# Turning two normalised tiles ahead of K's first half at the head of an attention kernel

## The chip, the cores and the metric

The kernel runs on one core of one Trainium2 chip. The metric is the device time of one execution in microseconds (us). Each execution also has a span: first to last instruction as the hardware profiler saw it, about 1.8 us shorter.

## The reference

Layer normalisation of x (2048 x 640), 32 heads of attention with head size 192 over given K and V caches, an output projection, and a gated feed-forward network whose silu scales the attention output. Everything is bf16.

```python
xn = _layernorm(x)
q = (xn @ wq)                       # per head: 2048 x 192
p = softmax(q @ k_cache.T * 192 ** -0.5)
s = concat_heads(p @ v_cache) @ wo
g = silu((silu(xn @ w1) * (xn @ w3)) @ w2)
return x + s * g
```

## The kernel before

One long stream of score and value products fills TensorE. In front of it stands a head of some 14 us, which loads, normalises and transposes what the first scores need. TensorE transposes by multiplying with an identity; the result goes to PSUM, the memory for TensorE's results (`pk` and `pst` in the timelines), and ScalarE or VectorE copies it out. In the timelines below ScalarE, VectorE and TensorE do their work in the order in which the program emits it (ScalarE, say: K at 9.00, the x tiles at 9.91). A load "lands" when its last byte has arrived. These are the parts of the head that the change touches:

```python
def turn_over(k):                   # products of the identity with itself: they keep TensorE's clock up
    for i in range(k):
        nc.tensor.matmul(warm, lhsT=ident_bf[:], rhs=ident_bf[:], start=True, stop=True)

def turn_k0(dst, half, sel):        # transposes of head 0's K, four per entry of sel     (L271)
def copy_k0(copy, src, half, two):  # copies half of them to KW                           (L277)
def ln_norm(g, i, engine):          # normalises tile i of x block g                      (L346)
def ln_turn(g, i2, copy):           # transposes two normalised tiles (L354), copies them to xnT (L356)
# ... cut ...
def head_start():
    load_x(0, 0, 2)
    load_x(0, 2, 4)
    load_k0(0, nc.sync)             # K, first half
    load_w0()
    turn_over(34)
    # ... cut: statistics of the four tiles; loads of K's second half, x block 1, V's first half ...
    for i in range(4):
        ln_norm(0, i, nc.vector)
    pk0 = ps_o.tile([P, 4, 512], BF16, tag="ob0", name="pk0")
    turn_k0(pk0, 0, range(4))                  # 16 transposes of K
    copy_k0(nc.scalar.copy, pk0, 0, 0)
    turn_over(4)
    ln_turn(0, 0, nc.scalar.copy)              # tiles 0 and 1
    turn_k0(pk1, 1, (0, 1))
    ln_turn(0, 1, nc.vector.tensor_copy)       # tiles 2 and 3
    swap_halves(0)
    copy_k0(nc.scalar.copy, pk0, 0, 1)
    copy_k0(nc.vector.tensor_copy, pk1, 1, 0)
    load_v(0, (1,))                            # V, second half
    load_x(2)                                  # the third block of x
    project_first()                            # first projection: q of head 0 (L391)
    turn_k0(pk1, 1, (2, 3))
    copy_k0(nc.scalar.copy, pk1, 1, 1)
    scores(0)                                  # first score products (L483)
    shift_first()                              # copies of q on VectorE (L400, L401)
    shift_k0()                                 # a copy of K on VectorE (L281)
    scores(1)
    ln_stats(1, 0)                             # statistics of the second block, then of the third (L316)
    # ... cut ...
```

## Time and profile before

| | before |
|---|---|
| time, median of the first 3 runs | 1941.45 us (1940.62 to 1942.42) |
| span of the profiled execution | 1939.6 us |
| TensorE busy | 1928.9 us |
| first projection product starts | 11.20 us |
| first score product starts | 14.06 us |

Three lines of the page of the kernel before: span, busy time of the engines, and, by engine, the chain of work that ended last (followed back from the last instruction to what each step waited for).

```profile
span 1939.6 us, 59659 instructions
...
PE 1928.9 (99%) x27267; PEld 1317.8 (68%) x27275; DVE 654.2 (34%) x997; ACT 1181.2 (61%) x1278; POOL 282.6 (15%) x501
...
PE 98%; DVE 1%; DMA 0%; ACT 0%; issue 0%; SPq 0%; POOL 0%; DVEq 0%; ACTq 0%
```

TensorE fills nearly all of the span and the chain. Only in the head can anything be won by moving work about.

The timeline of the head, cut to the instructions in question. Columns: start and duration in us, engine, line, operation, written tile <- read tiles, shape, number of instructions merged, and in brackets how long the engine was idle and what ended it.

```profile
2.77 3.81 PE L569 MATMUL pk<-ident_bf 128*128 128x128 bf16 x34 [2.77 <-POOL ident_bf masks.py:199]
...
7.14 0.79 DVE L346 TENSOR_SCALAR xn<-x_all,mv,rstd 128x640 bf16<-128x640 bf16 x2
...
7.90 1.07 PE L271 MATMUL pk<-ident_bf,kn 128*128 128x128 bf16 x16 [1.32 <-DMA kn<-in_A_k_cache_dram]
...
9.00 1.01 ACT L277 COPY KW<-pk 128x1024 bf16<-128x1024 bf16 x1 [2.85 <-PE pk L271]
9.03 0.72 PE L354 MATMUL pst<-ident_bf,xn 128*128 128x128 bf16 x10
...
9.91 1.23 ACT L356 COPY xnT<-pst 128x1280 bf16<-128x1280 bf16 x1
...
11.20 2.34 PE L391 MATMUL ps<-xnT,W 128*128 128x256 bf16 x20 [0.44 <-ACT xnT L356]
...
14.06 0.39 PE L483 MATMUL st<-qA,KW 128*128 128x512 bf16 x1
...
22.12 0.88 DVE L316 BATCH_NORM_STATS2 stats<-x_all 128x6 f32<-128x320 bf16 x2
```

The 34 products start 107 ns apart, the last at 6.27 (the 3.81 us also hold the end of the last one). The 16 transposes of K start when K lands and follow each other every 56 ns. ScalarE copies K first (9.00) and the two x tiles after it (9.91), and the first projection (11.20) waits for the second copy. The last line is VectorE's start on the third block of x.

The chain of waits of the kernel before, in its head (start, duration, what):

```profile
1.68 6.17 DMA kn<-in_A_k_cache_dram
7.90 1.08 PE pk L271 x16
9.00 1.01 ACT KW L277
10.02 1.14 ACT xnT L356
11.20 2.36 PE ps L391 x20
```

It says the same: the landing of K's first half, K's transposes, two copies on ScalarE, the projection.

### The profile page before, as it was taken

Reading aid. Unit: us, or ns where it says so; the run is one execution under the profiler, and the core shown is the slowest. Engines: PE = TensorE matmul, PEld = TensorE weight load, DVE = VectorE, ACT = ScalarE, POOL = GpSimd, SP = SyncE. Lnnn points to the kernel's source line nnn. Section 1 sums busy time; section 2 is a strip of 40 time slices with the busy share of each in tenths; the row PEclk is TensorE's granted clock in tenths of the full one; section 3 lists DMA queues with packets and bytes.
Section 4 is the critical chain, followed back from the end, with each engine's and each line's share of the span. In section 5 each row is a group of like instructions: output and inputs, shape, how many; then the busy total and the mean of one; then the engine's idle time right before and its main releaser. Section 6 shows DMA issues by size and latency. Waiting matters only on the chain.

```text
span 1939.6 us, 59659 instructions
## 1 busy us (share of the span) xinstructions
PE 1928.9 (99%) x27267; PEld 1317.8 (68%) x27275; DVE 654.2 (34%) x997; ACT 1181.2 (61%) x1278; POOL 282.6 (15%) x501
## 2 busy tenths in 40 slices
PE   8999999999999999999999999999999999999998
PEld 6666666666666666666666666666666666577776
DVE  7333333333333333333333333333333334521111
ACT  6667676767776767776777777677767677210000
POOL 3111111111111111111111111111111110000000
PEclk9999999999999999999999999999999999999999
DMA  8643433323233434363434343434333220937882
GB/s 178 132 101 64 101 68 83 86 56 91 58 89 65 98 63 99 68 162 68 101 64 101 68 101 68 100 66 100 69 68 90 63 70 2 259 70 135 152 152 61
DMA packets 394643, 178.98 MB, mean 92 GB/s; under 512 B 341616, under 2 KB 382832, under 8 KB 394384
## 3 DMA queue, kind: packets, MB, share of 16 engines
q1 hardware_dynamic: 371136, 125.32, 30.9%
q0 software_dynamic: 19472, 45.71, 9.8%
q8 instruction: 215, 3.52, 0.8%
q10 hardware_dynamic: 3776, 4.06, 0.7%
q14 instruction: 44, 0.36, 0.1%
HBM read 52.82 MB, written 27.79 MB: 42 GB/s over the span
## 4 chain that ended last, share of the span: by engine, by line
PE 98%; DVE 1%; DMA 0%; ACT 0%; issue 0%; SPq 0%; POOL 0%; DVEq 0%; ACTq 0%
PE obank L516 35%; PE st L487 33%; PE ps L424 14%; PE ps_s L111 11%; PE ps_f L728 3%; PE ps_gu L702 1%; PE st L488 1%; PE ps L410 0%; DMA kn<-in_A_k_cache_dram 0%; DVE stats L316 0%; PE ps L391 0%; DVE xn L346 0%; DVE mv L317 0%; DVE qA L429 0%; ACT xnT L356 0%
## 5 line engine op out<-in xcount | busy, mean ns | idle before, releaser
L490 ACT ACTIVATE pT<-st 128x1024 bf16<-128x1024 f32 x1024 | 1047.1, 1023 | 251.1 <-PE st L488 235.6
L516 PEld LDWEIGHTS <-pT 64*128 64x128 bf16 x16384 | 713.7, 94 | 242.2 <-ACT pT L490 0.2
L516 PE MATMUL obank<-vt,pT 64*128 64x193 bf16 x16384 | 851.8, 243 | 0.0
L487 PE MATMUL st<-qC,KW 64*128 64x512 bf16 x2046 | 605.6, 376 | 0.1
L525 DVE COPY osum<-obank 128x772 f32<-128x772 f32 x128 | 123.1, 962 | 788.8 <-PE obank L516 788.8
L488 PE MATMUL st<-qB,KW 64*128 64x512 bf16 x1024 | 385.0, 376 | 0.0
L487 PE MATMUL st<-qA,KW 64*128 64x512 bf16 x1022 | 384.3, 376 | 0.4 <-ACT pT L490 0.3
L488 PE MATMUL st<-qC,KW 64*128 64x512 bf16 x1022 | 384.3, 376 | 0.0
L488 PE MATMUL st<-qA,KW 64*128 64x512 bf16 x1022 | 384.3, 376 | 0.0
L487 PEld LDWEIGHTS <-KW 64*128 64x128 bf16 x3068 | 278.0, 94 | 153.8 <-issue 2.1
L424 PE MATMUL ps<-xnT,W 64*128 64x512 bf16 x1280 | 297.2, 376 | 0.0
L424 PE MATMUL ps<-xnS,W 64*128 64x512 bf16 x1280 | 296.3, 376 | 0.0
L488 PEld LDWEIGHTS <-KW 64*128 64x128 bf16 x3068 | 278.0, 94 | 0.7 <-issue 0.6
L377 POOL DMA_DIRECT2D qC<-qA x124 | 65.4, 528 | 1285.6 <-DVE rl_all L532 1270.0
L430 ACT CAST qB<-ps 128x512 bf16<-128x512 f32 x131 | 76.8, 586 | 228.3 <-PE ps L424 222.7
L111 PE MATMUL ps_s<-wo_sb,oT 128*128 128x384 bf16 (+3 forms) x1535 | 208.8, 299 | 0.1
L424 PEld LDWEIGHTS <-W 64*128 64x128 bf16 x2560 | 122.9, 94 | 121.2
L111 PEld LDWEIGHTS <-oT 128*128 128x128 bf16 x1536 | 148.4, 98 | 60.4
L526 DVE TENSOR_TENSOR osum<-osum,obank 128x772 f32<-128x772 f32 x128 | 122.7, 958 | 13.4
L533 DVE TENSOR_TENSOR ostage<-osum,rl_all 128x768 bf16<-128x768 f32 x128 | 122.7, 958 | 4.4
L465 DVE SCALAR_TENSOR_TENSOR hT<-pt,qB 64x512 bf16<-64x512 bf16 x64 | 43.8, 684 | 199.4 <-ACT pt L464 199.4
L429 DVE CAST qA<-ps 128x512 bf16<-128x512 f32 x131 | 90.5, 691 | 25.2 <-PE ps L410 7.2
(84 smaller groups left out, 622.4 us busy)
## 6 DMA issues: line engine op xcount, KB each, us to landing
o_scr<-ostage SPq DMA_DIRECT2D x16, 1536.0 KB, 10.3
vt<-in_A_v_cache_dram SPq DMA_DIRECT2D x63, 384.0 KB, 5.7
qC<-qA POOLq DMA_DIRECT2D x248, 64.0 KB, 1.9
qC<-qB POOLq DMA_DIRECT2D x124, 64.0 KB, 2.4
wo_sb<-in_A_wo_dram POOLq DMA_DIRECT2D x1, 7680.0 KB, 36.2
W<-in_A_wq_dram POOLq DMA_DIRECT2D x32, 160.0 KB, 3.4
W<-in_B_w_dram POOLq DMA_DIRECT2D x32, 80.0 KB, 3.2
W<-in_A_wq_dram POOLq DMA_DIRECT2D x32, 80.0 KB, 2.9
```

The lines of the kernel that those rows point to most:

```text
L111: nc.tensor.matmul(ps[:, 0:w], lhsT=oT[:, k, :], rhs=wo_sb[:, k, c0:c1], start=(k == 0), stop=(k == OC - 1))
L377: nc.gpsimd.dma_start(out=qC[0:64, half, :], in_=qAB[half][64:P, :])
L424: nc.tensor.matmul(ps[:, r * 512:(r + 1) * 512], lhsT=W[rows, j, :], rhs=xs[rows, j // 2, qs], start=(j == 0), stop=(j == 2 * DC - 1))
L429: a = nc.vector.tensor_copy(out=qAB[0][:], in_=ps[:, 0:512])
L430: b = nc.scalar.copy(out=qAB[1][:], in_=ps[:, 512:1024])
L487: nc.tensor.matmul(st2[:, 0:512], lhsT=ka, rhs=qa, start=r == 0 and nr == 3, stop=r == nr - 1)
L488: nc.tensor.matmul(st2[:, 512:1024], lhsT=kb, rhs=qb2, start=r == 0 and nr == 3, stop=r == nr - 1)
L490: nc.scalar.activation(out=pT2[:], in_=st2[:], func=ACT.Exp, scale=att_scale)
L516: nc.tensor.matmul(obanks[r][:, j * 256:j * 256 + DH + 1], lhsT=pT2[r * 64:(r + 1) * 64, t * 512 + j * P:t * 512 + (j + 1) * P], rhs=vt[r ...
L525: nc.vector.tensor_copy(out=osum[:], in_=ov[0])
L526: nc.vector.tensor_tensor(out=osum[:], in0=osum[:], in1=ov[1], op=ALU.add)
L533: nc.vector.tensor_tensor(out=ostage[:, qb * 4:qb * 4 + 4, hg * DH:(hg + 1) * DH], in0=osum[:, :, 0:DH], in1=rl.unsqueeze(2).to_broadcast( ...
```

## The change

The intent: turn the first two x tiles while K is still landing, let ScalarE copy them first, and keep TensorE busy with clock-keeping products until the first tile is normalised, so that the four filler products behind K's transposes are no longer needed.

```diff
-        turn_over(34)
+        turn_over(44)
 ...
         pk0 = ps_o.tile([P, 4, 512], BF16, tag="ob0", name="pk0")
+        ln_turn(0, 0, nc.scalar.copy)
         turn_k0(pk0, 0, range(4))
+        ln_turn(0, 1, nc.vector.tensor_copy)
+        turn_k0(pk1, 1, (0, 1))
+        swap_halves(0)
         copy_k0(nc.scalar.copy, pk0, 0, 0)
-        turn_over(4)
-        ln_turn(0, 0, nc.scalar.copy)
-        turn_k0(pk1, 1, (0, 1))
-        ln_turn(0, 1, nc.vector.tensor_copy)
-        swap_halves(0)
         copy_k0(nc.scalar.copy, pk0, 0, 1)
```

## The prediction

> **What bounds the kernel now.** The page shows TensorE busy for 1928.9 of 1939.6 us, and the chain of what ended last is 98% TensorE. The change can only act in the first 14 us of this; its real idle time lies there. The work behind it is unchanged, so at most part of the head can be won, under 0.1%.
>
> **The head, from the timeline.** The 34 clock-keeping products start at 2.77 us and are spaced 107 ns; the last one starts at 6.27. The transposes of K's first half start at 7.90, when that load lands (7.85), and are spaced 56 ns. The Trainium skill ("TensorE: Matmul & The Clock Gate", Part 1) gives the same two spacings for a throttled and a free array, 106.7 and 55.6 ns. The trace agrees; the clock opens between 6.4 and 7.9 us. On TensorE then follow in order: 16 K transposes, 4 filler products, 10 transposes of normalised tiles 0 and 1 (9.03), 8 K transposes, 10 of tiles 2 and 3 (10.03, last starts 10.54). ScalarE copies K out first (9.00, 1.01 us) and the first x tiles only after it (9.91, 1.23 us). So the first projection (L391) waits for that copy and starts at 11.20, with 0.44 us of TensorE idle. The chain of waits runs the same way.
>
> **What the change does.** Tiles 0 and 1 are normalised at 7.58 and 7.94. Their 10 transposes now go first, as K lands: last result about 8.45. ScalarE copies xnT at once, 8.5 to 9.7 instead of 9.91 to 11.14. TensorE: K's 16 about 8.3 to 9.15; tiles 2 and 3 (normalised by 9.07) to 9.7; VectorE copies them 9.9 to 10.7 instead of 10.79 to 11.62; 8 K transposes to 10.2. The projection can start at about 10.2, 1.0 us earlier. The 10 added products run where TensorE idles: 3 at 107 ns and 7 at 56, ending at about 7.3, ahead of the first norm; they cost nothing. ScalarE's two KW copies now follow the xnT copy (9.7 to 11.75), delaying its first cast of q a little but not the scores. First scores: about 13.1 instead of 14.06; first exponential about 14.0 instead of 15.05.
>
> **How much survives.** DMA does not speed up: the windows show it about fully busy from 10 to 22 us, so loads issued earlier land hardly earlier. The third block of x landed at 21.82 and VectorE began on it at 22.12, only 0.3 us later; behind it in VectorE's order stands the cast of the next q (23.16), for which TensorE waits at 23.86. The swapped x landed at 19.00 and is read at 20.07. So between 0.3 and 1.0 us should survive to the steady stage, where TensorE hides nothing and gives it all to the end. I expect about 0.7 us off: 1940.7 us, with 8 chances in 10 for 1939.4 to 1941.9. Faster by over 2%: 0.003; within: 0.99; slower: 0.007.
>
> **What would show it.** L354 before L271 on TensorE at about 7.6; L391 starting near 10.2; first L483 near 13.1; first L490 near 14.0; score matmuls at 36 us 0.3 to 1.0 us earlier.
>
> **What would make it wrong.** The clock opening late or closing again, so that the head runs at 107 ns (costing about 1 to 2 us); the projection held by another wait, such as the second K load (9.22); the third x load swallowing all the gain; run-to-run scatter above the effect.

## The result, and the profile after

| | before | after |
|---|---|---|
| median, 6 runs each | 1941.93 us (1940.62 to 1942.85) | 1941.61 us (1940.53 to 1941.92) |
| span of the profiled execution | 1939.6 | 1938.7 |
| first projection product | 11.20 | 10.31 |
| first score product | 14.06 | 13.26 |

The ratio is 0.9998, with a 95% interval of 0.9985 to 1.0011: the same. A ratio here is the mean time of one kernel's fast runs over that of the other's in the same rounds, so it is not quite the ratio of the medians quoted. By time alone nothing is seen. By the two profiles, the change won 0.9 us. But a profile shows one execution: the one of the changed kernel took 1940.53 us, the fastest of all its eleven (the other ten: 1941.37 to 1941.93), while the one of the kernel before took an ordinary 1941.37.

Two lines of the page of the kernel after:

```profile
span 1938.7 us, 59672 instructions
...
PE 98%; DVE 1%; DMA 0%; ACT 0%; issue 0%; POOL 0%; DVEq 0%; ACTq 0%
```

The timeline of its head, same columns:

```profile
2.77 4.81 PE L569 MATMUL pk<-ident_bf 128*128 128x128 bf16 x44 [2.77 <-POOL ident_bf masks.py:199]
...
7.27 0.79 DVE L346 TENSOR_SCALAR xn<-x_all,mv,rstd 128x640 bf16<-128x640 bf16 x2
...
7.76 0.81 PE L354 MATMUL pst<-ident_bf,xn 128*128 128x128 bf16 x10 [0.18 <-DVE xn L346]
...
8.41 1.06 PE L271 MATMUL pk<-ident_bf,kn 128*128 128x128 bf16 x16
8.61 1.23 ACT L356 COPY xnT<-pst 128x1280 bf16<-128x1280 bf16 x1 [2.29 <-PE pst L354]
...
9.73 1.94 ACT L277 COPY KW<-pk 128x1024 bf16<-128x1024 bf16 x2
...
10.31 2.35 PE L391 MATMUL ps<-xnT,W 128*128 128x256 bf16 x20
...
13.26 0.38 PE L483 MATMUL st<-qA,KW 128*128 128x512 bf16 x1 [0.16 <-DVE qA L393]
...
21.24 0.88 DVE L316 BATCH_NORM_STATS2 stats<-x_all 128x6 f32<-128x320 bf16 x2
```

The order is as intended: x tiles (7.76), K (8.41); ScalarE copies x at 8.61 and K's pieces at 9.73; the projection starts at 10.31 without any idle time in front. The chain of waits in the head of the kernel after:

```profile
0.75 2.97 DMA x_all<-in_A_x_dram
...
7.35 0.37 DVE xn L346
...
7.76 0.81 PE pst L354 x10
8.57 0.89 PE pk L271 x16
...
10.47 2.20 PE ps L391 x20
```

It starts at the landing of x, not of K, and runs through the statistics, the norms and TensorE's own row. Matching the same instruction in both traces, the first score product is 0.80 us earlier, and from 23.6 us to the last product every one is 0.88 us earlier: nothing is given back in this pair of profiles.

### The profile page after: what moved, and what is told of

Same layout as the page of the kernel before. It is cut to its first block, busy times and chain, and to the rows that moved or that the text cites. A ratio compares the mean times of both kernels' runs of the same rounds, so it can differ in the third digit from the quotient of the medians.

```text
span 1938.7 us, 59672 instructions
## 1 busy us (share of the span) xinstructions
PE 1929.6 (100%) x27273; PEld 1318.5 (68%) x27281; DVE 654.0 (34%) x997; ACT 1180.2 (61%) x1278; POOL 282.6 (15%) x501
## 4 chain that ended last, share of the span: by engine, by line
PE 98%; DVE 1%; DMA 0%; ACT 0%; issue 0%; POOL 0%; DVEq 0%; ACTq 0%
PE obank L516 35%; PE st L487 33%; PE ps L424 14%; PE ps_s L111 11%; PE ps_f L727 3%; PE ps_gu L701 1%; PE st L488 1%; DVE stats L316 0%; PE ps L410 0%; DMA x_all<-in_A_x_dram 0%; DVE xn L346 0%; PE ps L391 0%; PE pst L354 0%; DVE mv L317 0%; PE pk L271 0%
## 5 line engine op out<-in xcount | busy, mean ns | idle before, releaser
L429 DVE CAST qA<-ps 128x512 bf16<-128x512 f32 x131 | 90.5, 691 | 25.2 <-PE ps L410 7.3
```

The lines of the kernel that those rows point to most:

```text
L429: a = nc.vector.tensor_copy(out=qAB[0][:], in_=ps[:, 0:512])
```

## The experiments

Twelve kernels ran, on three chips, each with five timed rounds beside the kernel before (six times for before_28). Every interval of a ratio is about plus or minus 0.0013 wide, which is 2.5 us. So no ratio here tells two of these kernels apart. The profiles and the lists of single times are the evidence. "Third block" is the load of the third block of x, and "101st value product" is a fixed landmark in the stream, behind which the order of work is the same in all kernels.

### The two kernels again, and the change in halves

The kernel before and the kernel after were run unchanged. Two kernels take one half of the change each:

```diff
 order_only  = after  with  -turn_over(44)  +turn_over(34)
 warm_only   = before with  -turn_over(34)  +turn_over(44)
```

> The kernel before once more, to see what varies by itself. Theory A (the order: the gain of 0.88 us seen in the two profiles is the earlier copy of the first x tiles): the first projection product starts again within 0.25 us of 11.2 us, whatever the landing of K's first half, because K's transposes, ScalarE's copy of K and its copy of xnT stand in a row behind that landing. Theory L (luck of a load: K's first half landed at 7.85 in the profile before and at 7.36 after): with an early landing near 7.4 the projection starts near 10.8 and half the gain is gone. Theory C (clock): the opening of the clock differs from 6.7 us, and where it opens later than 8 us the transposes run at 107 ns and the projection starts after 12 us. Timed ratio 1.000 by construction.

> The changed kernel once more. Theory A: first projection near 10.3 us and the score matmuls of the steady stage 0.8 to 0.9 us ahead of a profile of the kernel before with the same clock and landings; timed 0.3 to 0.9 us less than before, ratio 0.9995 to 0.9998, which may not be clear of the scatter of about 1 us. Theory L: the projection start moves with the landing of K. Theory C: the times scatter less than those of before, and the clock opens before 8 us in every profile.

> The new order with the 34 clock-keeping products of before instead of 44. TensorE then has nothing between 6.4 us and the first norm at about 7.7 us. Theory A: the head is the same as after the whole change, first projection near 10.3 us, as long as the clock opens before 7.7. Theory C: the longer idle leaves the clock closed through the transposes: spacing 107 ns, first projection 1 to 2 us later, near 12 us, in some runs or all.

> The kernel before with 44 clock-keeping products in place of 34 and nothing else changed. Theory A: no gain, first projection 11.0 to 11.3 us; the last product ends at about 7.6 us, ahead of K's landing or up to 0.2 us after an early one. Theory C: most of the gain is here, steady stage 0.5 us or more earlier, and the spread of the times shrinks.

Measured, medians of 5 against 1941.27 us of the kernel before (9 runs): before_again 1941.22, after_again 1941.80, order_only 1941.28, warm_only 1941.80.

In this second profile of the kernel before, K's first half landed at 7.31 us, not 7.85, and the projection started at 10.65, not 11.20. So theory A's first forecast, 11.2 whatever the landing, failed. Theory L is right as far as it goes: in four profiles with the old order and an open clock (before, before_again, warm_only and, below, before_x2_early) the first score product comes 6.2 us after K's landing (7.85 to 14.06, 7.31 to 13.51, 7.45 to 13.65, 7.34 to 13.54). With the new order and many clock-keeping products it stands at 13.2 to 13.3 whether K lands at 5.68 or 7.68. So in these profiles the head gain is 0.2 to 0.85 us, depending on a landing, and the first pair had shown nearly its upper end. It may be less: in four other profiles (order_only, after_x2_early, turn_order_only, before_cold) K landed at 5.68 to 6.22, from the same issue at 1.68 or 1.69, and no profile shows the old order with so early a landing and an open clock.

In after_again that gain reached the first score product (13.21) and was gone at the 101st value product, which came at 30.43 against 30.35 in the first profile of before. VectorE's timeline in after_again:

```profile
22.20 0.89 DVE L316 BATCH_NORM_STATS2 stats<-x_all 128x6 f32<-128x320 bf16 x2 [0.93 <-DMA x_all<-in_A_x_dram]
...
23.24 0.64 DVE L429 CAST qA<-ps 128x512 bf16<-128x512 f32 x1
```

And TensorE's next work behind that cast, in the same run:

```profile
23.94 0.73 PE L354 MATMUL pst<-ident_bf,xn 128*128 128x128 bf16 x10 [0.87 <-DVE qA L429]
```

VectorE had nothing to do for 0.93 us, because the third block of x had not landed. Behind that in VectorE's row stands the cast of the next q (L429), for which TensorE waited 0.87 us. The chain of waits of the same run:

```profile
13.54 8.64 DMA x_all<-in_A_x_dram
```

VectorE's start on the third block in order_only:

```profile
21.95 0.89 DVE L316 BATCH_NORM_STATS2 stats<-x_all 128x6 f32<-128x320 bf16 x2 [0.55 <-DMA x_all<-in_A_x_dram]
```

There the wait was 0.55 us, and in warm_only 0.47. In the first profile of after it was zero, with 0.09 us to spare: landing at 21.15, start at 21.24.

The extra products by themselves (warm_only) do not move the head: the projection started 3.34 us after K's landing, as before. Nor did the times draw together, as theory C had it: they lie between 1941.45 and 1943.20. Without them (order_only) the projection started at 10.38, practically as after. In the profiled executions the clock opened in time in both.

### The third block loaded earlier

```diff
-        load_v(0, (1,))
-        load_x(2)
+        load_x(2)
+        load_v(0, (1,))
```

> The changed kernel with one swap: the load of the third x block is issued ahead of the second half of V, not behind it. Theory X (the change does win about 0.85 us, but in the runs where the third x block lands later than about 21.2 us VectorE waits for it and the gain is given back): the block lands between 19.7 and 21.0 us, VectorE's wait in front of the third block's statistics is zero, the 101st value product starts at the first score product plus 16.2 us, near 29.5, and the timed median falls 0.4 to 1.0 us below before, with less scatter. Rival theory A0 (the change wins nothing outside its first profile, for another reason): a median as before, 1941.2 to 1941.9, though the block lands early.

> The kernel before with the same swap of the two loads and nothing else. Theory X: before, VectorE reached the third block at 21.6 to 22.1 us by its own pace, so early data gain only in executions where the block lands later than that: 0 to 0.4 us in the median, and less than the swap gains in the changed kernel; first score product still 13.5 to 14.1 us. Rival: if loads alone set the time, the same 0.4 to 1.0 us as in the changed kernel.

Measured against 1941.12 us of before (9 runs, mean 1941.42): after_x2_early 1940.77 (mean 1941.06; single times 1940.51, 1940.75, 1940.77, 1941.45, 1941.84), before_x2_early 1940.87 (mean 1941.34; 1940.14, 1940.71, 1940.87, 1942.40, 1942.56). The timeline of after_x2_early, the two loads and VectorE's start on the third block:

```profile
12.46 1.77 SPq L214 DMA_DIRECT2D x_all<-in_A_x_dram  x1
...
14.27 0.90 SPq L289 DMA_DIRECT2D vt<-in_A_v_cache_dram  x1
...
21.31 0.88 DVE L316 BATCH_NORM_STATS2 stats<-x_all 128x6 f32<-128x320 bf16 x2
```

The block landed at 20.39, VectorE did not wait, and the 101st value product came at 29.54, 16.20 us after the first score product, as theory X had it. In before_x2_early the block landed only at 21.13, outside what I had expected of an early issue, but before VectorE reached it at 21.60; the head was unchanged (first score product 13.54). The means fell by 0.36 and 0.08 us. The median of after_x2_early fell by 0.35 us, just short of the 0.4 to 1.0 expected, that of before_x2_early by 0.25 (expected 0 to 0.4). The order between the two is the expected one, the sizes are within the scatter. Two of the five times of after_x2_early (1941.45, 1941.84) are as slow as the changed kernel's usual ones, and no profile shows why.

### Which of the two orders matters

copy_order_only leaves TensorE's order as before and lets ScalarE copy x first. turn_order_only has TensorE's new order and lets ScalarE copy K first.

```diff
 copy_order_only (against before)
-        copy_k0(nc.scalar.copy, pk0, 0, 0)
         turn_over(4)
         ln_turn(0, 0, nc.scalar.copy)
+        copy_k0(nc.scalar.copy, pk0, 0, 0)
 turn_order_only (against after)
-        ln_turn(0, 0, nc.scalar.copy)
+        first = []
+        ln_turn(0, 0, lambda out, in_: first.append((out, in_)))   # transposes only
         turn_k0(pk0, 0, range(4))
+        copy_k0(nc.scalar.copy, pk0, 0, 0)
+        nc.scalar.copy(out=first[0][0], in_=first[0][1])
 ...
         swap_halves(0)
-        copy_k0(nc.scalar.copy, pk0, 0, 0)
```

> The kernel before with TensorE's order kept, and ScalarE's copy of the first x tiles put ahead of its copy of K. The x tiles' transposes still stand behind K's and the four fillers, so the x copy can start only about 0.5 us after K's landing plus 1.4 us. Both theories of a joint effect: first projection only 0.1 to 0.25 us earlier than before at the same landing of K (start 3.1 to 3.25 us after the landing, where before it was 3.34), first score product about unchanged. If ScalarE's order alone made the gain: projection near 10.3 us.

> The changed kernel with TensorE's new order, but ScalarE copies K first and the x tiles second, as before. The x tiles are turned by 8.5 us and then wait for ScalarE's copy of K, which can start only at about 9.5. Joint effect: first projection near 11.6 us, later than before in both profiles, first score product near 14.6, the 101st value product near 30.8, time 0.3 to 1.0 us more than the kernel before. If TensorE's order alone made the gain: projection near 10.3 us.

The timeline of copy_order_only:

```profile
9.55 1.23 ACT L356 COPY xnT<-pst 128x1280 bf16<-128x1280 bf16 x1 [3.10 <-PE pst L354]
...
10.82 2.35 PE L391 MATMUL ps<-xnT,W 128*128 128x256 bf16 x20 [0.31 <-ACT xnT L356]
```

The timeline of turn_order_only:

```profile
7.94 0.81 PE L354 MATMUL pst<-ident_bf,xn 128*128 128x128 bf16 x10 [0.44 <-DVE xn L346]
...
9.68 1.01 ACT L277 COPY KW<-pk 128x1024 bf16<-128x1024 bf16 x1 [3.17 <-PE pk L271]
...
10.59 1.23 ACT L598 COPY xnT<-pst 128x1280 bf16<-128x1280 bf16 x1
...
11.87 2.34 PE L391 MATMUL ps<-xnT,W 128*128 128x256 bf16 x20 [1.22 <-ACT xnT L598]
```

turn_order_only has the x tiles turned early and does not copy them until 10.59, behind K. Its projection starts at 11.87, later than in either profile of before, with 1.22 us of TensorE idle. Its times, 1941.91 to 1942.11, hardly scatter; their median is 0.82 us over that of before (expected 0.3 to 1.0). In copy_order_only the x tiles are turned behind K, and the projection starts at 10.82 with K landed at 7.20. That is 3.62 us after the landing, more than the 3.1 to 3.25 expected; the clock opened only at 8.16 in this execution, and the first nine gaps between K's transposes were 82 to 108 ns in place of some 56, which is 0.4 us of it. Its first score product came at 13.78, no better than before. Its single times were 1940.47, 1940.98, 1942.36, 1942.48 and 1942.62 (mean 1941.78). So neither order alone gives the early projection; both together do.

### What a late clock costs

```diff
 after_cold  = after  with  -turn_over(44)  +turn_over(1)
 before_cold = before with  -turn_over(34)  +turn_over(1)
 before_28   = before with  -turn_over(34)  +turn_over(28)
```

> The changed kernel with one clock-keeping product in place of 44, to price a clock that opens late. Claim of the change (products must keep the clock up to the first norms): the 44 transposes ahead of the projection run at 107 ns in place of 56 ns (2.2 us more), the projection starts near 12.6 us and the first products of it are slow too; the clock opens between 10.5 and 14.5 us; first score product 15.5 to 18; time 2 to 4 us over the kernel before. Rival: the chain waits elsewhere anyway, and the late clock costs under 0.5 us.

> The kernel before with one clock-keeping product in place of 34. It prices a late clock for the old order. The kernel before shows two clusters of times, about 1941.1 and about 1942.6. If the upper one is executions in which the clock opens [...]after K's transposes began, this kernel should lie at or above the upper cluster, 1942.5 to 1944.5, with no execution near 1941. If the clock is not the cause of the upper cluster and costs nothing, the same 1941.1 with the same two clusters.

> The kernel before with 28 clock-keeping products in place of 34, ending near 5.8 us in place of 6.4. It asks where the upper cluster of the kernel before comes from: 1942.2 to 1942.9 in about a third of its executions, and in none of the changed kernel's. Theory C2 [...]: with a longer pause most executions, 3 to 5 of 5, land at 1942.2 to 1944, the clock opening between 9 and 12.6 us where the profiled one is such an execution; any other stays near 1941.1. Rival (the cluster comes from loads that land late): still about 1 or 2 of 5 above 1942.2, and a clock opening that does not go with them.

Measured: after_cold 1943.75 (1943.56 to 1944.20) and before_cold 1943.97 (1942.84 to 1944.66), both against 1941.41 of before. In the trace's clock record the clock opens at 13.35 and 11.69 us, and the first score products come at 15.86 and 15.44. So the clock-keeping products are worth some 2.3 to 2.6 us in either order; 34 of them already earn that in most executions. Of the price, 0.5 to 0.9 us fell late: TensorE waited once more, for the transposed rows of the third block in front of a later projection (L410), 0.90 us until 42.67 in after_cold and 0.48 until 41.91 in before_cold (the rows landed 0.25 and 0.24 us before; in before_cold the profile puts the wait down to an exponential that ended at 41.90).

The kernel before has 39 executions, 11 of them between 1942.3 and 1942.9 and the others between 1940.6 and 1942.2. The changed kernel has 11, none above 1941.93. before_28 was to tell whether that upper cluster is a late clock. Its profiled execution took 1942.62 us; the timeline of TensorE in it:

```profile
7.78 1.89 PE L271 MATMUL pk<-ident_bf,kn 128*128 128x128 bf16 x16 [1.83 <-DMA kn<-in_A_k_cache_dram]
...
9.88 1.27 PE L354 MATMUL pst<-ident_bf,xn 128*128 128x128 bf16 x10
...
11.47 0.72 PE L354 MATMUL pst<-ident_bf,xn 128*128 128x128 bf16 x10
```

The 16 transposes of K take 1.89 us, 107 ns each, and only the last ten (11.47) are all at 56 ns; the clock record opens at 11.10. The first score product comes at 15.33. So an execution with a late clock does land in the upper cluster. But the count went against theory C2, that a longer pause behind the products makes most executions slow: only 2 of 6 executions lay above 1942.2, not 3 to 5 of 5, beside 4 of 10 of the kernel before on the same chip. Whether the upper cluster of the kernel before itself is late clocks is therefore not shown: no profile caught one of its slow executions.

### A version meant to beat both

x2_pool is after_x2_early with two copies moved from VectorE's row to GpSimd, which has nothing to do there.

```diff
     def shift_k0():
-        nc.vector.tensor_copy(out=KW[0:64, 3, :], in_=KW[64:P, 0, :])
+        nc.gpsimd.tensor_copy(out=KW[0:64, 3, :], in_=KW[64:P, 0, :])
     def shift_first():
-        nc.vector.tensor_copy(out=qC[0:64, 0, :], in_=qAB[0][64:P, :])
+        nc.gpsimd.tensor_copy(out=qC[0:64, 0, :], in_=qAB[0][64:P, :])
 ...
         copy_k0(nc.vector.tensor_copy, pk1, 1, 0)
-        load_v(0, (1,))
+        shift_k0()
         load_x(2)
+        load_v(0, (1,))
 ...
         shift_first()
-        shift_k0()
```

> A version that should beat both: the changed kernel, the third x block loaded ahead of V's second half, and two copies that stand in VectorE's row ahead of the second block's statistics (the shifted K, 0.42 us, and one half of the shifted q, 0.29 us) given to GpSimd, idle there. Theory (from 12.7 us on VectorE's row is what the steady stage waits for, unless the third block lands late): the second block's statistics start about 0.6 us earlier relative to the first score product, and the 101st value product comes about 15.6 us after the first score product in place of 16.2, unless the third block (19.7 to 21.0) now lands too late for it; timed 0.6 to 1.4 us under before. Rival: scores wait for GpSimd's slower copies, or VectorE and GpSimd hinder each other, and nothing is gained.

Measured: 1940.46 us (1940.29 to 1940.76) against 1941.41 (1940.96 to 1942.80); ratio 0.9994, interval 0.9981 to 1.0008. The five single times lie all below the nine of before. The timeline of x2_pool:

```profile
11.60 1.03 POOL L281 COPY KW<-KW 64x1024 bf16<-64x1024 bf16 x1 [1.15 <-ACT KW L277]
...
13.12 0.73 POOL L401 COPY qC<-qA 64x512 bf16<-64x512 bf16 x1 [0.48 <-DVE qA L393]
...
13.41 0.59 DVE L400 COPY qC<-qA 64x512 bf16<-64x512 bf16 x1
...
14.03 0.89 DVE L316 BATCH_NORM_STATS2 stats<-x_all 128x6 f32<-128x320 bf16 x2
```

The same copy in after_x2_early, where GpSimd copies nothing:

```profile
13.54 0.29 DVE L400 COPY qC<-qA 64x512 bf16<-64x512 bf16 x1
```

The third block landed at 20.53 and VectorE reached it at 20.82, 7.62 us after the first score product in place of 7.98. The hope of 0.6 us was cut twice. First, VectorE's remaining copy (L400) took 0.59 us in place of 0.29 while GpSimd made its own copy. The Trainium skill ("SBUF — State Buffer", "SBUF: two separate sides") says that VectorE and GpSimd share a port pair under an exclusive lock, in some of VectorE's modes. The trace fits that: L400 ended at 14.00, 0.15 us behind GpSimd's copy; which mode VectorE was in, no run shows. Secondly, of those 0.36 us only 0.12 reached the 101st value product (16.08 us after the first score product in place of 16.20), since TensorE, which in the other kernels waits for VectorE there, now began the next transposes (22.79) 0.29 us after VectorE's cast had ended (22.50), with 0.1 us of pause behind the value products, and had become the limit itself. How the rest of the lower times divides between the loads' order and scatter is not shown.

### All profiles in one table

Times in us, read from the traces of the profiled executions. "Clock opens" is the start of the first entry of the trace's clock record.

| kernel | clock opens | first score product | third block lands | VectorE starts on it (idle before) | 101st value product | span |
|---|---|---|---|---|---|---|
| before | 6.73 | 14.06 | 21.82 | 22.12 (0) | 30.35 | 1939.60 |
| before_again | 6.85 | 13.51 | 21.11 | 21.57 (0) | 29.80 | 1938.99 |
| after | 7.38 | 13.26 | 21.15 | 21.24 (0) | 29.47 | 1938.67 |
| after_again | 6.47 | 13.21 | 22.18 | 22.20 (0.93) | 30.43 | 1939.67 |
| order_only | 5.82 | 13.34 | 21.92 | 21.95 (0.55) | 30.18 | 1939.42 |
| warm_only | 6.82 | 13.65 | 22.25 | 22.27 (0.47) | 30.50 | 1939.74 |
| after_x2_early | 8.13 | 13.34 | 20.39 | 21.31 (0) | 29.54 | 1938.74 |
| before_x2_early | 6.89 | 13.54 | 21.13 | 21.60 (0) | 29.83 | 1939.10 |
| copy_order_only | 8.16 | 13.78 | 21.19 | 21.75 (0) | 29.98 | 1939.21 |
| turn_order_only | 7.21 | 14.73 | 21.60 | 22.79 (0) | 31.02 | 1940.28 |
| after_cold | 13.35 | 15.86 | 21.53 | 23.84 (0) | 32.07 | 1942.42 |
| before_cold | 11.69 | 15.44 | 21.23 | 23.51 (0) | 31.74 | 1941.59 |
| before_28 | 11.10 | 15.33 | 22.22 | 23.39 (0) | 31.62 | 1940.85 |
| x2_pool | 5.87 | 13.20 | 20.53 | 20.82 (0) | 29.28 | 1938.52 |

One rule fits all rows but x2_pool, which took work out of VectorE's row: VectorE starts on the third block at the later of two times, 8.0 to 8.1 us after the first score product, or the block's landing; 8.23 us after that start comes the 101st value product. And in every row but the two cold ones the span ends 1909.2 to 1909.3 us after that product (the cold ones took 0.6 and 1.1 us longer, mostly in the wait at L410 told above). So the span of a profiled execution with an open clock, to 0.1 us, is set by whichever of these two came last.

## Why the prediction was right or wrong

**The range and the class were right.** 1941.61 us lies in 1939.4 to 1941.9, and the kernel is neither faster nor slower by 2%. That much is luck: the range also holds 1941.45, the time of the kernel before, so no gain at all would have landed in it, and the point of 1940.7 was 0.9 us too low.

**The mechanism in the head was right.** L354 went first (7.76; predicted 7.6), the projection started at 10.31 (10.2), the first score product at 13.26 (13.1), the first exponential at 14.24 (14.0). copy_order_only and turn_order_only show that it takes both orders.

**The clock was right in its effect.** I let 7 of the 10 added products run at 56 ns; nearly all ran at 107, because the clock opened at 7.38. They still ended before the first tile was ready (TensorE stood idle for 0.18 us in front of L354), and cost nothing in that execution.

**"How much survives: between 0.3 and 1.0 us, about 0.7" is the term that failed**, in two ways. First, the 1.0 us by which the projection was to start earlier was counted against a single landing of K, at 7.85 us. That landing is not a constant: it was 7.31, 7.34 and 7.45 in three other profiles of the old order with that load unchanged, where the head gain to the first score product is 0.2 to 0.4 us. Secondly, I had named the third block as a possible limit with only 0.3 us of margin, and then let it cost a part of the gain. It took 0.93 us of VectorE's time in the second profile of the changed kernel, which swallowed the whole. The statement that "loads issued earlier land hardly earlier" held: with the original order of the loads the third block was issued between 13.5 and 16.2 us and landed between 21.1 and 22.3, and the earliest issue landed among the latest. Putting it in front of another load brought it to 20.39 and 20.53, and in before_x2_early only to 21.13.

**The steady time.** The kernel before has 39 executions with a mean of 1941.56 us, and the changed kernel 11 with a mean of 1941.59. The difference of 0.88 us between the first two profiles was real in those two executions and is not what the change does on average. What it does show is less spread: no execution above 1941.93 against 11 of 39 above 1942.3. The lists of the other kernels tell what this goes with. Where TensorE turns K first, as before, 19 of 60 executions lie above 1942.2 us (before 11 of 39, warm_only 1 of 5, before_x2_early 2 of 5, copy_order_only 3 of 5, before_28 2 of 6). Where it turns the x tiles first (after, order_only, after_x2_early, turn_order_only, x2_pool), none of 31 does; the slowest took 1942.11. The two cold kernels are left out. So the slow executions go with TensorE's order. Neither the ten added products nor the order of the loads nor ScalarE's order removed them by itself. Whether a late clock or a late K makes them is not shown.

**What stays open.** The changed kernel's typical execution (1941.4 to 1941.9) is slower than the lower cluster of the kernel before (27 executions from 1940.6 to 1941.7, mean 1941.12); the two means agree only because the upper cluster is gone. A late third block explains it in the one profile of the changed kernel that shows it, and in order_only, a relative of it; the executions without a profile leave no landing times. Why that load lands anywhere between 21.1 and 22.3 us is settled by half. The traces show that with the original order of the loads it landed 1.56 to 1.66 us after V's second half, which stands in front of it on the same queue, in ten of eleven profiles (before_cold: 1.85), whenever it had been issued. With the loads swapped, V's second half landed 1.29 to 1.31 us after it. That fits a load which takes its turn behind the other one, and says why an earlier issue alone did not help. Why that one landed anywhere between 19.4 and 20.7 us stays open.

## What to carry to other kernels

Before you price a gain in the head of a kernel against a load's landing, take several profiles: a landing of one execution is a sample, and the gain you read off may be its scatter. The execution that was profiled may also be the fastest of its kernel, as here: look where its time stands in the list of times. A step taken off the critical path is worth only the margin to the next limit, so put a number on that margin and change it together with the step (here: issue the third block before a load that is needed later). When one effect lies far below the scatter of the times, find a landmark in the stream behind which all kernels do the same work, and compare the times at which they reach it.

## What the Trainium skill lacked or had wrong

- "TensorE: Matmul & The Clock Gate", Part 1, gives 106.7 and 55.6 ns between products of 128 columns with a closed and an open clock. The traces agree: 107 and 56 ns. It also says that the opening varies by 500 ns either way between runs, since its window runs freely. Here it varied more: it fell anywhere from 5.82 to 8.16 us in the kernels with 34 or 44 products, which all started them at 2.77 or 2.78.
- The same page, Part 4, says of TensorE's transpose mode that it does not count as activity for the clock in the way products do. Here the transposes did: in before_cold TensorE made one product at 2.78 us, 16 transposes of K from 6.27, 4 products from 7.95 and then transposes only, and the clock opened at 11.69, ahead of the projection (12.58). In before_28 the transposes behind the opening (11.10) ran at 56 ns. The trace lists them as MATMUL, so it doesn't say whether they ran in the mode that the page means. The measurement decides for this kernel's transposes.
- No page that I read says that the granted clock read from a trace may count as full before the first opening. Here before_28, whose clock record starts with the opening at 11.10 us, has a mean of 1.00 over its first 10 us, in which its instructions are spaced 107 ns. For the head of a kernel, read the spacing of equal instructions, not the granted clock.
- "SBUF — State Buffer" states the lock between VectorE and GpSimd but gives no cost for a small copy. Here a 64 x 512 bf16 copy on VectorE took 0.59 us in place of 0.29 beside a GpSimd copy of 0.73 us.
- "Trainium Kernel Development and Optimization" ("Key Constraints") says that all queues run on the same 16 DMA engines and interleave. It gives no number for what an earlier issue is worth when they are full. Here a 640 KB load issued at 13.54 us landed at 22.18, and one issued at 14.73 landed at 21.11.
